# Attention and two MLPs on one core: float64 weights converted in pairs, first MLP cut into even and odd blocks

## The chip, the cores and the metric

The kernel runs on one core of one Trainium2 chip. The metric is the device time of one execution in microseconds (us). The engines are called PE (TensorE), DVE (VectorE), ACT (ScalarE), POOL (GpSimd) and SP (SyncE); SP issues the DMAs of this kernel.

## What is computed

Inputs are `x` (8 batches, 8 heads, 512 rows, 64 columns) and `state` (8, 8, 32, 64), both float32, and four float64 weights. Cross attention in both directions gives 4608 rows of 512; two MLPs without bias follow, one with a squared ReLU, one with ELU:

```python
scores = scale * np.matmul(x, state.transpose(0, 1, 3, 2))
...
xread = np.matmul(a, state)
scores2 = scale * np.matmul(state, x.transpose(0, 1, 3, 2))
...
sread = np.matmul(a2, x)
return np.concatenate([xread, sread], axis=2).astype(np.float32)
...
h = x @ w_in
r = np.maximum(h, 0.0)
g = r * r
return (g @ w_out).astype(np.float32)
...
h = x @ w_in
g = np.where(h > 0.0, h, alpha * (np.exp(np.minimum(h, 0.0)) - 1.0))
return (g @ w_out).astype(np.float32)
```

(What is left out are the two softmaxes, with the maximum subtracted and 1e-9 added to the sum, that give a and a2 from the scores.) In the kernel the weights of the first MLP are `w1` and `v1`, those of the second `w2` and `v2`. A "block" is one batch: 512 rows of `x`; the 32 state rows of all batches are one block of their own.

## The kernel before

**Products.** Every operand of a large matmul is split into a high part (HI, rounded to fp32r) and the rest (LO), and each product is three matmuls, HI·LO, HI·HI and LO·HI (`mm3`, L158 to L160, and `product`, L43). The split is an ACT copy and a DVE subtraction (`split`, L163 and L164).

**Weights.** The four weights arrive as float64 and are turned into float32 on the chip. `load64` loads a raw tile (128 partitions, 512 numbers of 8 bytes, 512 KB) by one DMA on SP, into one of `RAW` = 4 buffers. `convert` needs two ACT steps (L210 on the high words, L212 on the low words) and four DVE steps (L214 clamp, L215 shift, L217 add, L219 sign). A `w1` piece is written into a resident tile. A `v1` piece goes into one of `CV` = 4 buffers `cv`, is stored to DRAM (`d_v`), and is split into a resident tile (L236 on ACT, L238 on DVE).

**Seven products for four.** Where two blocks are taken together, a 2x2 block product is formed from seven products instead of eight (`out_products`, `first_product`). This needs sums of weight blocks, made on DVE (`sums`, into the buffer `tf`, L247 and following), split into `wf` (L260 on ACT, two buffers) and stored to DRAM (`f_w`, `f_v`) by `put_split`; the pair stages load them again as `wr`. For `v1` they are made by `sums_v1` from `d_v` (steps called "f1"), which also stores the split tiles (`p_v`); for `w2` and `v2` by `conv_pair`.

**Stages.** The start: attention of block 0 (scores `sc`, maximum `mx` at L362, exponential at L364, transposes, the operand `at` split at the end), the first `w1` pieces, and small filler matmuls (`idle`, L517). Then blocks 0 to 5 one at a time (`block`): 16 steps f over DFF; each has 6 matmuls `h` from `at` and `m` (the product of `w1` and the state, made by `emit_m` from 16 small matmuls `mp`, L331), relu and square on ACT (L469 to L473) and a DVE subtraction (L474), and, `LAG` = 2 steps later, 12 matmuls `acc` with `v1`. A list `bg` hangs other work on the steps: `next_conv` (a step of each conversion in progress, then perhaps a new one; a load follows when a conversion is over), the attention of the next block, its loads, and the reading of the state (`sr`, `srt`). Block 0 converts `w1` and `v1` while it uses them, and begins the f1 sums; blocks 1 to 5 finish those and convert `w2` and `v2`. Blocks 6 and 7 are a `pair` (h1 in place of h, then `out_products`); the state's rows of the first MLP follow, then the second MLP in four pairs and its state rows.

**Order.** A scheduler orders each engine's instructions by what is written and by estimates of its own; the written order gives priorities. `tc.issue_after` holds an instruction behind another one (`gate`, `pace`). DMAs on SP are issued in SP's order, and each waits for its buffer there.

## Time and profile before

| | us |
|---|---|
| median of 3 runs (lowest, highest) | 1353.0 (1352.66, 1353.6) |
| span of the profiled execution | 1350.5 |
| PE busy | 1327.5 (98%) |
| DVE busy | 951.0 (70%) |
| ACT busy | 839.5 (62%) |
| first h of block 0 / of block 1 | 27.7 / 128.2 |
| first h1 of the pair | 510.7 |

The span is the profiled execution's own time from its first to its last instruction; the runs' time has 2.5 us more around it. A row of the timeline reads: start, duration, engine, line, operation, output<-input, shapes, count, and in brackets the idle time of that engine before it and what ended it. Line numbers are those of the kernel before.

### The profile page before, as it was taken

The numbers are of one execution on the slowest core, as the hardware profiler recorded it, in microseconds if no ns is written. First come the engines' busy times: TensorE is split into PE (matmuls) and PEld (weight loads), VectorE is DVE, ScalarE is ACT, GpSimd is POOL, SyncE is SP. The second block draws the span as 40 slices with busy tenths as digits, with TensorE's granted clock in tenths as the row PEclk, the third lists the DMA queues.
The fourth block names the chain that finished last, engine by engine and source line by source line (L and its number), as shares of the span: only waits on it lengthen the run. The fifth ranks groups of instructions, "written<-read, shape, count | busy, mean of one in ns | idle before, by whom it ended". The sixth has DMA issues, their size and how long they took to land.

```text
span 1350.5 us, 19746 instructions
## 1 busy us (share of the span) xinstructions
PE 1327.5 (98%) x7064; PEld 1057.1 (78%) x7064; DVE 951.0 (70%) x1437; ACT 839.5 (62%) x1417; POOL 0.7 (0%) x6
## 2 busy tenths in 40 slices
PE   8989999999999999999999999999999999999998
PEld 6656777777777776778988888888888888888898
DVE  6997868686878865775576884579636884568644
ACT  5887758676777657644467843676446743666444
POOL 0000000000000000000000000000000000000000
PEclk9999999999999999999999999999999999999999
DMA  6988856575857424279077777767776777778732
GB/s 240 318 300 310 305 178 230 201 267 190 279 197 266 151 82 153 97 255 349 25 252 208 224 240 224 208 194 247 229 225 194 206 210 223 209 204 284 226 110 100
DMA packets 127729, 290.72 MB, mean 215 GB/s; under 512 B 13840, under 2 KB 22032, under 8 KB 124560
## 3 DMA queue, kind: packets, MB, share of 16 engines
q1 hardware_dynamic: 127632, 289.46, 66.3%
q8 instruction: 56, 0.92, 0.3%
q14 instruction: 41, 0.34, 0.1%
HBM read 212.86 MB, written 76.55 MB: 214 GB/s over the span
## 4 chain that ended last, share of the span: by engine, by line
PE 89%; DMA 5%; DVE 3%; ACT 3%; issue 1%; SPq 0%; ACTq 0%; DVEq 0%
PE x L43 16%; PE X L43 13%; PE z L43 8%; PE Z L43 6%; PE acc L158 6%; PE acc L159 6%; PE acc L160 6%; PE h L158 5%; PE h L159 4%; PE h L160 4%; PE y L43 4%; PE Y L43 3%; DMA raw_v<-in_v_dram 2%; PE mp L331 2%; PE hs L43 2%; PE as L43 2%
## 5 line engine op out<-in xcount | busy, mean ns | idle before, releaser
L163 ACT ACTIVATE gp<-g 128x1024 fp32r<-128x1024 f32 (+1 forms) x168 | 154.0, 917 | 146.0 <-PE x L43 69.5
L164 DVE TENSOR_TENSOR gp<-g,gp 128x1024 fp32r<-128x1024 f32 (+1 forms) x168 | 174.9, 1045 | 95.4 <-ACT gp L163 94.4
L43 PE MATMUL x<-gp,wr 128*128 128x512 f32 x960 | 223.5, 390 | 0.0
L43 PEld LDWEIGHTS x<-gp,wr 128*128 128x128 f32 x960 | 179.7, 188 | 39.4 <-ACT eu L71 1.9
L43 PE MATMUL X<-xf,wr 128*128 128x512 f32 x768 | 186.7, 390 | 0.0
L43 PEld LDWEIGHTS X<-xf,wr 128*128 128x128 f32 x768 | 143.4, 188 | 31.7 <-ACT u L748 1.3
L158 PE MATMUL acc<-gs,v 128*128 128x512 f32 x384 | 154.4, 402 | 3.8 <-DVE gs L474 1.9
L159 PE MATMUL acc<-gs,v 128*128 128x512 f32 x384 | 150.4, 392 | 0.0
L160 PE MATMUL acc<-gs,v 128*128 128x512 f32 x384 | 150.2, 392 | 0.0
L43 PE MATMUL z<-gp,wr 128*128 128x512 f32 x480 | 110.4, 389 | 0.0
L744 DVE SCALAR_TENSOR_TENSOR g<-r,g 128x512 f32<-128x512 f32 x96 | 63.9, 689 | 65.8 <-ACT r L743 65.8
L43 PEld LDWEIGHTS z<-gp,wr 128*128 128x128 f32 x480 | 90.1, 188 | 18.7
L158 PE MATMUL h<-at,m 128*128 128x512 f32 x256 | 103.0, 403 | 1.7 <-ACT r L469 1.7
L158 PEld LDWEIGHTS acc<-gs,v 128*128 128x128 f32 x384 | 72.0, 188 | 38.1 <-issue 15.9
L160 PE MATMUL h<-at,m 128*128 128x512 f32 x256 | 100.7, 395 | 0.5 <-ACT m L346 0.5
L159 PE MATMUL h<-at,m 128*128 128x512 f32 x256 | 101.0, 395 | 0.0
L43 PE MATMUL Z<-xf,wr 128*128 128x512 f32 x384 | 97.4, 389 | 0.0
L469 ACT ACTIVATE r<-h 128x512 f32<-128x512 f32 x96 | 57.1, 595 | 64.4 <-PE h L160 64.1
L742 ACT ACTIVATE r<-g 128x512 f32<-128x512 f32 x96 | 57.5, 625 | 57.5 <-DVE g L821 40.4
L160 PEld LDWEIGHTS acc<-gs,v 128*128 128x128 f32 x384 | 72.1, 188 | 19.8 <-issue 4.2
L159 PEld LDWEIGHTS acc<-gs,v 128*128 128x128 f32 x384 | 72.2, 188 | 18.6 <-issue 3.4
L43 PEld LDWEIGHTS Z<-xf,wr 128*128 128x128 f32 x384 | 72.1, 188 | 15.0
(145 smaller groups left out, 2173.6 us busy)
## 6 DMA issues: line engine op xcount, KB each, us to landing
wr<-f_v SPq DMA_DIRECT2D x256, 256.0 KB, 3.0
wr<-f_w SPq DMA_DIRECT2D x224, 256.0 KB, 2.9
f_v<-wf SPq DMA_DIRECT2D x40, 512.0 KB, 3.3
raw_w<-in_w_dram SPq DMA_DIRECT2D x32, 512.0 KB, 4.8
raw_v<-in_v_dram SPq DMA_DIRECT2D x32, 512.0 KB, 5.0
f_w<-wf SPq DMA_DIRECT2D x24, 512.0 KB, 2.8
xt<-in_xt_dram SPq DMA_DIRECT2D x8, 1024.0 KB, 6.9
xn<-in_xn_dram SPq DMA_DIRECT2D x8, 1024.0 KB, 6.1
```

Of the source, the lines that this page charges most:

```text
L43: nc.tensor.matmul(ps, wk[a], xk[b], start=start and k == 0 and i == 0, stop=last and k == len(w) - 1 and i == 2, skip_group_check=True)
L158: mm(ps, w[HI], x[LO], start=first, stop=False)
L159: mm(ps, w[HI], x[HI], start=False, stop=False)
L160: mm(ps, w[LO], x[HI], start=False, stop=last)
L163: copy = nc.scalar.activation(out=hi, in_=src, func=AF.Copy)
L164: nc.vector.tensor_tensor(out=lo, in0=src, in1=hi.bitcast(F32), op=ALU.subtract)
L331: mm(ps[e][32 * k:32 * k + 32, :], st_t[b][r, k, :], x(k, r), start=True, stop=True)
L469: pace[:] = [nc.scalar.activation(out=r, in_=ps, func=AF.Relu)]
L742: act(out=r, in_=h, func=AF.Relu, scale=-1.0)
L744: nc.vector.scalar_tensor_tensor(out=out, in0=r, scalar=-1.0, in1=h, op0=ALU.add, op1=ALU.max)
```

## The change

Raw tiles hold two pieces (1024 numbers, 1 MB), in three buffers instead of four; `cv` holds a pair, two buffers instead of four. The steps of a conversion are half as many and twice as wide, and so are the `v1` splits and the stores `d_v` and `p_v`. The next load is written right behind a conversion's last step. `load_x(0)` comes first, and the first loads are two `w1` pairs and one `v1` pair. Block 0 begins only conversions of `w1` and `v1`; f1 starts in block 1. The sums are made in place in the `cv` tile; `tf` is gone, `wf` has one larger buffer. Of the four blocks that `out_products` works on in the first MLP, two were the lower and upper half of DFF; they are the even and the odd f blocks now, so that the two v1 pieces of one pair belong together. `PLACE` and `columns` say where a form or a column lies, and the host lays out the four weights accordingly.

```diff
-RAW, CV = 4, 4
+RAW, CV = 3, 2
+PLACE = {1: 0, 2: 1, 3: 2, 7: 3, 5: 4, 4: 5, 6: 6}
...
-                  tf=pool("tf", 1),
-                  wf=pool("wf", 2))
-    wo_p = pool("wo", FC)
+                  wf=pool("wf", 1))
+    wo_p = pool("wo", HF)
...
-        def load64(name, i):
+        def load64(name, j):
...
-            t = conv_p["raw"].tile([P, 512, 2], I32, name=f"raw_{name}{i}", tag="raw")
-            nc.sync.dma_start(out=t.rearrange("p f w -> p (f w)"), in_=src64[name][i].bitcast(I32))
+            t = conv_p["raw"].tile([P, 1024, 2], I32, name=f"raw_{name}{j}", tag="raw")
+            nc.sync.dma_start(out=t.rearrange("p f w -> p (f w)"),
+                              in_=src64[name][j].rearrange("p r f -> p (r f)").bitcast(I32))
...
             nc.vector.scalar_tensor_tensor(out=bits, in0=high, scalar=SIGN, in1=bits, op0=ALU.bitwise_and, op1=ALU.bitwise_or)
+            next_load()
...
+        def conv_v1(j):
+            v = conv_p["cv"].tile([P, 2, 512], F32, name="cv", tag="cv")
+            yield from convert("v1", j, v)
+            d = wd["v1", j] = dram.tile([P, 2, 512], F32, name=f"d_v1{j}", tag=f"d_v1{j}")
             nc.sync.dma_start(out=d, in_=v)
-            t = wo_p.tile([P, 2, DM], F32R, name=f"v1_{f}", tag="wo")
+            t = wo_p.tile([P, 2, 2, DM], F32R, name=f"v1_{j}", tag="wo")
...
+        def put_split(w, src):
+
+            n = src.shape[1]
+            h = conv_p["wf"].tile([P, n, 2, 256], F32R, name="wf", tag="wf")
+            with tc.issue_after(pace[0].ins):
+                nc.scalar.activation(out=h[:, :, HI], in_=src, func=AF.Copy)
+            nc.vector.tensor_tensor(out=h[:, :, LO], in0=src, in1=h[:, :, HI].bitcast(F32), op=ALU.subtract)
+            nc.sync.dma_start(out=w, in_=h.bitcast(F32))
+
+        def sums(q):
+
+            b12, b11, b21, b22 = (q[:, i] for i in range(4))
+            sub = lambda out, x, y: nc.vector.tensor_tensor(out=out, in0=x, in1=y, op=ALU.subtract)
+            sub(b11, b12, b11)
+            sub(b12, b22, b12)
+            yield
+            sub(b22, b22, b11)
+            sub(b21, b21, b22)
+            yield
...
+            q = v.rearrange("p r (c f) -> p (r c) f", c=2)
+            put_split(w[:, :3], q[:, 1:])
+            yield
+            yield from sums(q)
+            put_split(w[:, 3:], q)
...
+        def columns(f, k):
+            c = k if f % 2 else (k + 2) % KC
+            return slice(c * P, (c + 1) * P)
+
+        pieces = [("w1", 0), ("w1", 1)]
+        for i in range(HF):
+            pieces += [("v1", i)] + ([("w1", i + 2)] if i < HF - 2 else [])
...
+        def advance():
+            for c in list(busy):
+                if next(c[0], busy) is busy:
+                    busy.remove(c)
+
+        def begin():
+            held = sum(n != "w1" for _, n in busy)
+            if converting and (converting[0][0] == "w1" or held < CV):
...
-        next_load()
         load_x(0)
-        for _ in range(RAW - 1):
+        for _ in range(RAW):
             next_load()
         load_xn(0)
...
+        def first_weights():
+            advance()
+            if converting[0][0] in ("w1", "v1"):
+                begin()
...
             if b == 0:
-                for i in range(FC - 1):
-                    at(i, next_conv)
-                    at(i, next_conv)
+                for i in range(FC + LAG):
+                    at(i, advance)
+                    at(i, first_weights)
...
-                t = g[(11, 12, 21, 22)[s // HF]]
-                if f % 2 == 0:
+                t = g[(11, 12, 21, 22)[s // FC * 2 + f % 2]]
+                if f % 4 < 2:
```

Three places show what this does to the order on the engines. The first is DVE at the very start, the conversion of the first `w1` tile and the maxima `mx0` of block 0's scores. Before:

```order
L214 TENSOR_SCALAR w1_00_154<-w1_00_154 128x512
L215 TENSOR_SCALAR w1_00_154<-w1_00_154 128x512
L217 ISA w1_00_154<-raw_w10_140,w1_00_154 128x1024
L219 SCALAR_TENSOR_TENSOR w1_00_154<-raw_w10_140,w1_00_154 128x512
L362 TENSOR_REDUCE mx0_180<-sc0_0_182 128x1
L362 TENSOR_REDUCE mx0_180<-sc0_1_183 128x1
```

Now:

```order
L213 TENSOR_SCALAR w1_00_149<-w1_00_149 128x1024
L214 TENSOR_SCALAR w1_00_149<-w1_00_149 128x1024
L216 ISA w1_00_149<-raw_w10_141,w1_00_149 128x2048
L218 SCALAR_TENSOR_TENSOR w1_00_149<-raw_w10_141,w1_00_149 128x1024
L361 TENSOR_REDUCE mx0_175<-sc0_0_177 128x1
L361 TENSOR_REDUCE mx0_175<-sc0_1_178 128x1
```

The same four steps stand ahead of `mx0`, on a tile of twice the size; on SP, whose order was raw_w10, st0, xt0, raw_w11, raw_w12, raw_w13, xn0, it is st0, xt0, raw_w10, raw_w11, raw_v10, xn0 now. A little further on DVE's row has the scaling of the state's read-out, `srs0`, ahead of the split of `at0`; it stood in block 0 before.

The second is PE in block 2, the small matmuls `mp3_2` that prepare `m` for block 3, between `h` and `acc`. Before:

```order
L160 MATMUL h_3062<-at3_2548,m3_11_2906 128x512
L331 MATMUL mp3_2_0_3076<-w1_20_489,st3_1574 32x512
L331 MATMUL mp3_2_1_3077<-w1_20_489,st3_1574 32x512
L331 MATMUL mp3_2_0_3076<-w1_20_489,st3_1574 32x512
L331 MATMUL mp3_2_1_3077<-w1_20_489,st3_1574 32x512
L331 MATMUL mp3_2_0_3076<-w1_21_615,st3_1574 32x512
L331 MATMUL mp3_2_1_3077<-w1_21_615,st3_1574 32x512
L331 MATMUL mp3_2_0_3076<-w1_21_615,st3_1574 32x512
L331 MATMUL mp3_2_1_3077<-w1_21_615,st3_1574 32x512
L158 MATMUL acc_2942<-gs_2969,v1_3_484 128x512
```

Now:

```order
L160 MATMUL h_2712<-at3_2244,m3_11_2576 128x512
L330 MATMUL mp3_2_0_2726<-w1_20_466,st3_1334 32x512 x2
L330 MATMUL mp3_2_0_2726<-w1_21_561,st3_1334 32x512 x2
L158 MATMUL acc_2606<-gs_2633,v1_1_416 128x512
L159 MATMUL acc_2606<-gs_2633,v1_1_416 128x512
L330 MATMUL mp3_2_1_2727<-w1_20_466,st3_1334 32x512 x2
L330 MATMUL mp3_2_1_2727<-w1_21_561,st3_1334 32x512 x2
L160 MATMUL acc_2606<-gs_2633,v1_1_416 128x512
```

One group became two, with two `acc` matmuls between them. The scores `sc3`, in the same block range, were split into a first matmul and seven others in the same way; in block 0 the small groups stand in 11 places, where they stood in 14.

The third is ACT where block 5 ends and the pair begins: `o` copies block 5's result, `m6_1` is the first split of the pair's second `m`, `g1` its first relu. Before:

```order
L260 ACTIVATE wf_5176<-tf_4896 128x2x256
L260 ACTIVATE wf_5180<-cv_4789 128x2x256
L503 ACTIVATE o_5196<-acc_4498 128x512
L260 ACTIVATE wf_5208<-tf_5004 128x2x256
L163 ACTIVATE m6_10_5282<-mp6_1_0_5272 128x512
L503 ACTIVATE o_5202<-acc_4500 128x512
L163 ACTIVATE m6_11_5285<-mp6_1_1_5273 128x512
L260 ACTIVATE wf_5212<-tf_5004 128x2x256
L630 ACTIVATE g1_5260<-h1_5253 128x512
```

Now:

```order
L502 ACTIVATE o_4649<-acc_4032 128x512
L502 ACTIVATE o_4655<-acc_4034 128x512
L163 ACTIVATE m6_10_4727<-mp6_1_0_4717 128x512
L163 ACTIVATE m6_11_4730<-mp6_1_1_4718 128x512
L632 ACTIVATE g1_4704<-h1_4697 128x512
```

The `wf` splits of the last weight sums moved to earlier places, and none is left there. On PE the row was mp6_1, mp6_2, h1; it is mp6_1, 36 matmuls of h1, mp6_2.

## Rows read from the trace of the kernel before

**Rows 1.** Page part 1: busy us, share of the span, instructions of each engine.
```profile
PE 1327.5 (98%) x7064; PEld 1057.1 (78%) x7064; DVE 951.0 (70%) x1437; ACT 839.5 (62%) x1417; POOL 0.7 (0%) x6
```

**Rows 2.** Windows: stretch, us, busy PE, PEld, DVE, ACT, POOL, PEclk, DMA share, GB/s.
```profile
9.14:10.00 0.86, 0.86 (x16) 0.18 (x16) 0.00 (x0) 0.00 (x0) 0.00 (x0) 1.00 1.01 414
27.70:128.20 100.50, 92.55 (x516) 59.55 (x515) 90.95 (x180) 83.23 (x153) 0.00 (x0) 0.98 0.88 302
28.30:117.70 89.40, 81.59 (x470) 50.86 (x469) 82.93 (x164) 77.12 (x142) 0.00 (x0) 0.99 0.88 295
128.20:205.00 76.80, 76.80 (x455) 58.48 (x453) 54.38 (x104) 47.91 (x89) 0.00 (x0) 1.00 0.69 245
```

**Rows 3.** Waits of DVE, 28.3 to 117.7: line, releaser, us, times, longest.
```profile
DVE cv L214 <- ACT cv L210: 5.2, 5, 1.3
```

**Rows 4.** Waits of ACT in the same stretch.
```profile
ACT cv L210 <- DMA raw_v<-in_v_dram: 7.5, 5, 2.5
```

**Rows 5.** Timeline of the start: PE, DVE, ACT, SP.
```profile
9.14 1.09 PE L331 MATMUL sc<-xt,st 64*32 64x512 f32 x16 [0.38 <-DMA xt<-in_xt_dram]
...
10.31 1.29 DVE L362 TENSOR_REDUCE mx<-sc 128x1 f32<-128x512 f32 x2 [2.72 <-PE sc L331]
...
18.16 1.06 ACT L376 ACTIVATE t<-t 128x1024 f32<-128x1024 f32 x1 [0.56 <-DVE t L375]
...
30.84 0.69 ACT L210 ACTIVATE cv<-raw_v 128x512 f32<-128x512 f32 x1
...
32.27 1.10 PE L411 MATMUL sr<-xn,a2t 128*32 128x64 f32 x64
...
35.69 0.33 SPq L234 DMA_DIRECT2D d_v<-cv  x1
```

**Rows 6.** Groups by shape, DVE, 28.3 to 117.7: count, busy us, mean ns, idle before.
```profile
L219 DVE SCALAR_TENSOR_TENSOR cv<-raw_v,cv 128x512 int32<-128x512 int32 x16 | 11.0, 685 | 0.1
L238 DVE TENSOR_TENSOR v<-cv,v 128x512 fp32r<-128x512 f32 x16 | 10.9, 682 | 0.0
...
L214 DVE TENSOR_SCALAR cv<-cv 128x512 f32<-128x512 f32 x16 | 6.7, 422 | 5.2 <-ACT cv L210 5.2
...
L375 DVE TENSOR_TENSOR t<-t,m 128x1024 f32<-128x1024 f32 x1 | 1.2, 1217 | 0.0
```

**Rows 7.** Timeline of DVE, two neighbours in the start.
```profile
23.68 1.24 DVE L390 STREAM_TRANSPOSE atf<-t 128x1024 f32<-128x1024 f32 x1
24.84 0.65 DVE L219 SCALAR_TENSOR_TENSOR w<-raw_w,w 128x512 int32<-128x512 int32 x1
```

**Rows 8.** Timeline of PE around a split group in block 0.
```profile
56.32 1.04 PE L331 MATMUL sc<-xt,st 64*32 64x512 f32 x2
57.30 0.74 PE L160 MATMUL h<-at,m 128*128 128x512 f32 x2
```

**Rows 9.** Timeline of PE and ACT at the change from block 5 to the pair.
```profile
504.94 1.09 PE L331 MATMUL mp<-w,st 64*32 64x512 f32 x16
...
505.98 0.63 ACT L260 ACTIVATE wf<-tf 128x512 fp32r<-128x512 f32 x1 [2.37 <-DMA f_v<-wf]
...
507.99 2.81 PE L331 MATMUL mp<-w,st 64*32 64x512 f32 x16 [1.96 <-DVE m L164]
...
510.73 0.79 PE L158 MATMUL h<-at,m 128*128 128x512 f32 x1
...
512.17 0.39 PE L158 MATMUL h<-at,m 128*128 128x512 f32 x1
```

**Rows 10.** Window of the same place, columns as in rows 2.
```profile
508.70:512.10 3.40, 3.40 (x18) 1.38 (x18) 1.38 (x3) 0.14 (x1) 0.00 (x0) 0.51 0.93 357
```

**Rows 11.** DMA issues, 0 to 30, then 30 to 120: count, KB, median us to landing.
```profile
xn<-in_xn_dram SPq DMA_DIRECT2D x1, 1024.0 KB, 11.8
...
raw_v<-in_v_dram SPq DMA_DIRECT2D x14, 512.0 KB, 5.6
...
xn<-in_xn_dram SPq DMA_DIRECT2D x2, 1024.0 KB, 6.5
```

More of the change, by code (lines that the diff above doesn't have):

```diff
@@ L299, in attn_mlp_kernel @@
+        pieces = [("w1", 0), ("w1", 1)]
+        for i in range(HF):
+            pieces += [("v1", i)] + ([("w1", i + 2)] if i < HF - 2 else [])
         pairs2 = [(name, j) for name in ("w2", "v2") for j in range(HF)]
         converting = pieces + [("f1", j) for j in range(HF)] + pairs2
[L301 to L302 removed]
+        loading, busy = iter(pieces + pairs2), []
         def next_load():
@@ L307, in next_load @@
                 load64(*x)
-        def next_conv(more=True):
-            for c, name in list(busy):
-                if next(c, busy) is not None:
-                    busy.remove((c, name))
-                    for _ in range({"w1": 1, "v1": 1, "f1": 0}.get(name, 2)):
-                        next_load()
-            held = sum({"w1": 0, "v1": 1}.get(n, 2) for _, n in busy)
-            if more and converting and (converting[0][0] == "w1" or held + (converting[0][0] != "v1") < CV):
+        def advance():
[5 more added lines that the diff above has]
+            if converting and (converting[0][0] == "w1" or held < CV):
                 name, i = converting.pop(0)
@@ L523, in attn_mlp_kernel @@
         gate.append(A[0]["exp"])
-        for _ in range(3):
-            next_conv()
+        next_conv()
+        advance()
         gate.clear()
@@ L530, in attn_mlp_kernel @@
         at_soft2(0)
-        for _ in range(4):
-            next_conv(False)
+        while busy:
+            advance()
         with busy_pe(8):
```

121 lines of the change are left out of this document (45 added, 76 removed).

## The prediction

> **What bounds the kernel now.** I read the page's busy shares first: PE is busy 1327.5 us of a span of 1350.5 [rows 1], so where PE is full only fewer or shorter matmuls help, and their number stays at 7064. The gain or loss must come from the 23 us in which PE has nothing, or from the price of single PE pieces. Then the windows by stage [rows 2]: block 0, from its first h at 27.7 to block 1's first at 128.2, takes 100.5 us with PE busy 92.55, so 8 of the 23 us lie there; block 1 has no such hole (76.8 of 76.8). In block 0 the engine behind PE is DVE: from 28.3 to 117.7, where the last v1 piece is split, it is busy 82.93 of 89.4 us, PE 81.59, and the DMA share is 0.88. After 117.7 PE is at full pace for the last 10.5 us. So block 0 lasts as long as DVE's chain of conversions plus those 10.5 us. DVE's waits say what is late when DVE stands still: 5.2 of its 6.5 us of idle time are ACT's first conversion step [rows 3], and ACT there waits 7.5 us for raw_v [rows 4]: late loads, passed on. A second place is the change from block 5 to the pair of blocks 6 and 7, below.
>
> **Term 1, the start: +4.0.** Before, the first load is half a megabyte and DVE's four steps on it are over when the scores arrive; PE starts on them at 9.14 as xt lands, and mx follows on DVE at 10.31 [rows 5]. Afterwards w1_00 is 1 MB and third in SP's queue, and DVE's order has its four steps ahead of mx, so mx and all of block 0's softmax wait for it. Until xt lands the queue has moved 1.56 MiB before, and must move 2.06 MiB until w1_00 is in: 0.5 MiB more at the 414 GB/s of that moment [rows 2] is 1.3 us, so it is in at 10.4. ACT's first step on 1024 columns takes 1.06, as on t at 18.16 [rows 5]: 11.5. DVE's four steps on 1024 columns have no rows as such; L219 takes 0.68 on 512 columns and a 1024-wide step of the softmax 1.22 [rows 6], 0.53 more; L217 is taken as L219. L214 takes 0.42 and runs at twice the elements per time, so 0.27 more, 0.69; L215 as L214. Together 0.69 + 0.69 + 1.22 + 1.22 = 3.8, and mx starts at 15.2 instead of 10.3: +4.9. Behind it one pair is converted (3.8) where three pieces were (3 x 2.2 = 6.6): -2.8. The state's read-out sr0 (1.1 on PE at 32.27, [rows 5]), its scaling and its transpose now stand ahead of at0's split and so of the first h; with the hops between the engines, 1.8. Sum +3.9, taken as 4.0; bounds 3.0 (sr0 fits into a wait of PE) and 5.5 (nothing of the 2.8 comes back, since those pieces stood between steps of the softmax that wait for ACT anyway, less what sr0 hides).
>
> **Term 2, block 0: -7.6.** On DVE, 28 conversions of four steps and 16 splits become 14 and 8 of double width. Durations: 28 x (0.42 + 0.42 + 0.68 + 0.685) = 61.7 becomes 14 x 3.81 = 53.3, and 16 x 0.68 = 10.9 becomes 8 x 1.22 = 9.7: 9.6 us less in 64 fewer instructions. But instructions that stand in a row overlap: L390 starts at 23.68 and takes 1.24, and the next starts at 24.84, 1.16 after it [rows 7], so each costs some 0.08 less than its duration, and 64 x 0.08 = 5.1 of the 9.6 were never paid. Net -4.5; in what follows -4.6, as the f1 sums, a step or two of which stand in block 0 now, leave it. Of the idle 6.5 us I take 3.0 away: the f1 transfers (cv<-d_v and p_v<-v) leave block 0, and a load is issued behind the last step of a conversion. Bounds: no idle left, -11.1; the same idle, -4.6; 10 us of idle, -1.1. Below -12.6 PE itself ends it: 92.55 less three splits fewer of its mp pieces (3.2) and sr0's 1.5 that moved ahead is 87.9. Half the idle is in between because the loads are as many bytes as before and each lands later.
>
> The Trainium skill, "VectorE: DVE Perf Modes", section "The TRN2 errata", says that a VectorE operation on SBUF pays a fixed cost per instruction, (N+151)/0.96 ns for an fp32 tensor_tensor, and advises wide tiles. The durations agree (685 and 1217 ns at 512 and 1024 columns [rows 6]); charged in full for each instruction saved, it would give about 10 us here instead of 4.6, and the starts in [rows 7] speak against that.
>
> **Term 3, pieces of PE in blocks 2 and 3: +2.1.** The new order splits two groups of 16 small matmuls that ran whole: the scores in block 2 and the third mp in block 3. A whole group of 16 takes 1.09 [rows 5]. A split-off part costs nearly as much: at 56.32, in block 0, two matmuls of sc take 1.04 and the next h starts 0.98 after them [rows 8], though 2 of 16 would be 0.14. With the first matmul behind it a little longer, 1.07 for each: 2 x 1.07 = 2.1, on PE, which has nothing to hide it. Bounds 1.6 and 2.2.
>
> **Term 4, block 5 to the pair: -4.0.** Behind block 5's last acc, mp6_1 starts at 504.94, and h is at full pace only from 512.17 [rows 9], 7.2 us later, where two mp (1.09 each) and three h (1.44 at half pace from 510.73 on, so 0.7) need 2.9. In between ACT's wf waits 2.37 for the transfer of the wf before it, m6_1 stands behind that wf on ACT, PE waits 1.96 for m, and then runs at 0.51 of its clock, the 1.2 GHz level, from 508.7 to 512.1 [rows 10]. The new order has no wf near m6_1: the last weight sums are long over, and PE goes from mp6_1 to h1. So 7.2 - 2.9 = 4.3; I take 4.0. Bounds -4.3, and -2.0 if a copy of acc keeps m6_1 late enough for the lower clock to return.
>
> **Edits at nothing.** One wf buffer instead of two makes ACT wait for the landing of the previous f transfer in blocks 1 to 4, as it waits 2.37 at 505.98 now [rows 9]; r and gs stand behind it on ACT, and PE's acc behind gs. LAG 2, with two steps of matmuls between h and its acc, covers a wait of that size, and ACT and DVE are busy only 47.91 and 54.38 of 76.8 us in block 1 [rows 2]. If that cover is gone, +2 (one such wait). The exchange of halves and even blocks, PLACE and columns leave numbers, sizes and dependences of the matmuls as they are: 0.
>
> **Sum.** 4.0 - 7.6 + 2.1 - 4.0 = -5.5. The profiled span is 1350.5; the median of the runs, 1353.0, has 2.5 us more around it, which the change doesn't touch. 1353.0 - 5.5 = **1347.5**.
>
> **Rivals.** A: the loads stop holding up DVE, as with twice the bytes per load fewer transfers have to be waited for; with the start at its lower bound, 3.0 - 11.1 + 2.1 - 4.0 = -10.0: 1343.0. For it: three pairs are underway ahead, where four pieces were. Against it: a load's landing grows with its bytes, xn's 1 MB taking 6.5 us and the 512 KB pieces 5.6 [rows 11]. The Trainium skill, "DMA: Bandwidth & Descriptors", section "Bandwidth", asks for 1 MiB and more per transfer to reach three quarters of the peak, which speaks for A; but at 9.14, with half-megabyte loads behind xt, the rate was 414 GB/s already [rows 2].
>
> B: the loads stay as late as they are, and DVE's 6.5 us idle stay, with the start at +5.0: 5.0 - 4.6 + 2.1 - 4.0 = -1.5: 1351.5. The same time comes out if term 4 fails alone. For it: the DMA share of 0.88.
>
> C, slower: the three buffers of 1 MB become the loop that sets block 0. A buffer is free again after landing plus conversion. At my forecast a pair takes 81.8 / 14 = 5.84 us, so a buffer is wanted again after 17.5. Now a piece is held from ACT's first step at 30.84 to the store of its cv at 35.69, 4.9 us [rows 5]; a pair twice that, 9.7. With xn's landing of 6.5 [rows 11] the loop is 16.2 and just fits. With xn's 11.8 in the start [rows 11] it is 21.5. Taken a little over half way, 10.0, it is 19.7: 2.2 more for each of 13 / 3 turns, +9.5: 1357.0. It makes the kernel slower than before by more than 0.2% from a loop of 19.4 on, that is from landings of 9.7. Against it: without f1's transfers block 0 moves fewer bytes.
>
> **How the numbers follow.** Forecast 0.43, A 0.14, B 0.27, C 0.16. Differences within 0.2%, or 2.7 us, are what a measurement of this kernel can't tell from none. Forecast and A lie under 1350.3, but for a little of the forecast's upper end (0.02); B lies within; C above 1355.7. Faster 0.55, same 0.29, slower 0.16. The range reaches from 1342.5, A's time, to 1356.0, short of C.
>
> **What would show it.** Mx at about 15 and the first h at about 32 for term 1 (under 30 would refute it). From the first h to block 1's first, some 93 us for term 2, with about 3.5 us of DVE idle behind ACT's first step; over 100 would be C, with ACT waiting for raw tiles more than the 9 us of now. Two more short groups of L330 in blocks 2 and 3. At the pair, about 3.5 us from the last acc to h at full pace, with no time at the lower clock. The prediction is wrong if ACT's waits for raw_v grow, or if a wait for the one wf buffer puts r behind PE's need in blocks 1 to 4.

## The result and the profile after

The changed kernel takes 1359.84 us (median of 6 runs, 1357.52 to 1365.0) against 1353.3 (6 runs, 1352.23 to 1354.4): a ratio of 1.0056, 95% interval 1.0040 to 1.0072. It is slower by 0.56%, where 1347.5 was forecast; the time lies above the range of 1342.5 to 1356.0. The profiled execution took 1359.61, with a span of 1357.8, 7.3 more than before.

Where the 7.3 us of span arise is read from PE's timeline: the first h of each block in both kernels (us from the span's start).

| | before | after | gained (-) or lost (+) in the stretch that ends here |
|---|---|---|---|
| first h of block 0 | 27.73 | 29.98 | +2.25 (forecast +4.0) |
| first h of block 1 | 128.20 | 128.39 | -2.06 (forecast -7.6) |
| first h of block 2 | 202.38 | 202.57 | 0.00 |
| first h of block 5 | 424.92 | 435.30 | +10.19 (forecast +2.1) |
| last acc of block 5 ends | 505.01 | 515.11 | -0.28 |
| first h of the pair | 510.73 | 516.91 | -3.92 (forecast -4.0) |
| first X of the second MLP | 691.12 | 697.22 | -0.08 |
| last matmul | 1345.91 | 1353.26 | +1.25 |

(Block 1's first h is that of [rows 2]; the last window there, to 205.00, reaches 2.6 us into block 2.) So the loss is made in blocks 2 to 4, where the kernel before had no hole. The +1.25 in the second MLP is left out of what follows: the stretch from the first X to the state's last rows took 586.6 us in the kernel before, e1, e3 and e4 below, and 587.8 to 588.1 in the changed kernel, e7 and e14, with the same instructions there in all of them. The three longer ones have a stretch at the lower clock where that MLP begins, and the four shorter ones have none; in the changed kernel it is this window (columns of [rows 2]), behind a wait of 2.25 us for a weight. It is not the whole answer, as e2 took 587.8 us there without one.

```profile
696.50:700.00 3.50, 3.34 (x8) 2.70 (x9) 3.29 (x3) 0.46 (x1) 0.00 (x0) 0.51 0.93 300
```

Page part 1 of the changed kernel, to be held against [rows 1]: fewer and longer instructions on DVE and ACT, and PE busy 2.5 us more with the same 7064 matmuls.

```profile
PE 1330.0 (98%) x7064; PEld 1060.8 (78%) x7064; DVE 941.3 (69%) x1261; ACT 833.8 (61%) x1305; POOL 0.7 (0%) x6
```

The start, from the timeline of the changed kernel, against [rows 5]: w1_00 is in at 8.8, its four steps come ahead of mx, and mx starts at 13.96. Xt, issued at 1.18, took 5.1 us to land (last line, DMA issues from 0 to 14), so it was in at 6.3; PE came to the scores only at 8.72, behind its filler matmuls.

```profile
8.72 1.09 PE L330 MATMUL sc<-xt,st 64*32 64x512 f32 x16
...
8.81 1.16 ACT L209 ACTIVATE w<-raw_w 128x1024 f32<-128x1024 f32 x1 [6.48 <-DMA raw_w<-in_w_dram]
...
10.00 0.69 DVE L213 TENSOR_SCALAR w<-w 128x1024 f32<-128x1024 f32 x1 [10.00 <-ACT w L209]
...
12.82 1.23 DVE L218 SCALAR_TENSOR_TENSOR w<-raw_w,w 128x1024 int32<-128x1024 int32 x1
13.96 1.28 DVE L361 TENSOR_REDUCE mx<-sc 128x1 f32<-128x512 f32 x2
...
xt<-in_xt_dram SPq DMA_DIRECT2D x1, 1024.0 KB, 5.1
```

Block 0, windows with the columns of [rows 2]: from its first h to block 1's, and DVE's stretch of conversions, which answers to 28.30 to 117.70 there.

```profile
29.98:128.39 98.41, 88.65 (x449) 59.37 (x449) 83.19 (x108) 79.20 (x111) 0.00 (x0) 0.97 0.84 296
...
30.65:118.00 87.35, 77.59 (x401) 50.24 (x400) 78.10 (x99) 73.03 (x103) 0.00 (x0) 0.96 0.83 288
```

DVE is busy 78.10 us there instead of 82.93, and idle 9.25 instead of 6.5. What DVE waited for, and what ACT did, against [rows 3, 4]:

```profile
DVE w L213 <- ACT w L209: 2.7, 2, 2.1
DVE cv L213 <- ACT cv L209: 2.2, 1, 2.2
DVE gs L473 <- ACT gs L472: 1.6, 3, 1.1
```

```profile
ACT m L343 <- PE mp L330: 6.1, 2, 4.5
ACT cv L209 <- DMA raw_v<-in_v_dram: 2.0, 1, 2.0
ACT w L209 <- DMA raw_w<-in_w_dram: 1.6, 2, 0.9
```

ACT's wait for raw_v is down from 7.5 us to 2.0 (its second step, on the other word, waits 1.3 more for the same tile), but a wait for m's small matmuls, up to 4.5 at once, has come.

Blocks 2 to 4 as one window, first the kernel before, then the changed one:

```profile
202.38:424.92 222.54, 222.54 (x1327) 169.24 (x1326) 171.80 (x330) 158.82 (x297) 0.00 (x0) 1.00 0.65 228
```

```profile
202.57:435.30 232.73, 228.75 (x1328) 170.41 (x1326) 181.59 (x277) 162.09 (x256) 0.00 (x0) 0.99 0.67 243
```

Before, PE was busy all of the 222.54 us. Now it takes 10.2 us more: 4.0 of waiting and 6.2 of longer busy time for the same matmuls. Of the 6.2, the two groups that are split now are 2.0, the lower clock in block 3 (below) is 1.7, and a third mp group, which takes 2.19 us in block 4 where a whole one takes 1.09, is 1.1. DVE has 9.8 us more to do in this stretch. Counted by the splits into `wf` on ACT, the sums of 14 pairs of w2 and v2 stand in it (28 wide splits, two for each pair), where it was 12 (48 narrow ones, four for each). PE's waits in it, and ACT's for DMAs:

```profile
PE acc L158 <- DVE gs L473: 1.6, 2, 1.2
PE acc L158 <- ACT o L502: 1.0, 1, 1.0
PE mp L330 <- DVE t L365: 0.9, 1, 0.9
PE sc L330 <- DVE m L164: 0.4, 1, 0.4
```

```profile
ACT raw_v L211 <- DMA raw_v<-in_v_dram: 9.1, 6, 3.0
ACT raw_w L211 <- DMA raw_w<-in_w_dram: 7.9, 3, 4.4
ACT wf L245 <- DMA f_w<-wf: 5.5, 5, 2.0
```

The waits of PE are few, short and of four kinds. ACT's waits for raw tiles are no news by themselves: in the kernel before they came to 14.2 us in the same blocks, with 2.4 more for wf, while PE never waited:

```profile
ACT raw_v L212 <- DMA raw_v<-in_v_dram: 7.8, 6, 2.4
ACT raw_w L212 <- DMA raw_w<-in_w_dram: 6.4, 6, 2.4
```

One of PE's waits as an example, in block 3 (timeline of PE):

```profile
301.68 0.40 PE L159 MATMUL acc<-gs,v 128*128 128x512 f32 x1
302.98 1.06 PE L330 MATMUL mp<-w,st 64*32 64x512 f32 x8 [0.90 <-DVE t L365]
303.97 0.79 PE L160 MATMUL acc<-gs,v 128*128 128x512 f32 x1
304.56 0.63 PE L158 MATMUL acc<-gs,v 128*128 128x512 f32 x1
...
307.12 0.54 PE L158 MATMUL acc<-gs,v 128*128 128x512 f32 x1
307.50 0.39 PE L159 MATMUL acc<-gs,v 128*128 128x512 f32 x1
```

Here the second half of the split mp3_2 waits 0.90 us for a transpose that DVE makes late; then seven matmuls take 0.63 or more instead of 0.39, and the granted clock is 0.66 of full speed on average over 303 to 308: part of that stretch ran at the lower of its two levels, 1.2 GHz, and the rest at 2.4.

At the pair (timeline of PE), against [rows 9]: h1 follows mp6_1 with a wait of 0.78, at full pace.

```profile
515.04 1.09 PE L330 MATMUL mp<-w,st 64*32 64x512 f32 x16
516.91 0.50 PE L158 MATMUL h<-at,m 128*128 128x512 f32 x1 [0.78 <-ACT o L502]
517.25 0.40 PE L159 MATMUL h<-at,m 128*128 128x512 f32 x1
```

### The profile page after: what moved, and what is told of

The parts are those of the page before. It is cut to its first block, busy times and chain, and to the rows that moved or that the text cites. A ratio compares the mean times of both kernels' runs of the same rounds, so it can differ in the third digit from the quotient of the medians.

```text
span 1357.8 us, 19168 instructions
## 1 busy us (share of the span) xinstructions
PE 1330.0 (98%) x7064; PEld 1060.8 (78%) x7064; DVE 941.3 (69%) x1261; ACT 833.8 (61%) x1305; POOL 0.7 (0%) x6
## 4 chain that ended last, share of the span: by engine, by line
PE 86%; ACT 4%; DMA 4%; DVE 3%; issue 1%; SPq 0%; ACTq 0%; DVEq 0%
PE x L44 16%; PE X L44 13%; PE z L44 8%; PE Z L44 6%; PE acc L158 6%; PE acc L160 5%; PE acc L159 5%; PE h L158 4%; PE y L44 4%; PE h L160 4%; PE h L159 4%; PE Y L44 3%; PE mp L330 2%; PE hs L44 2%; PE as L44 2%
## 5 line engine op out<-in xcount | busy, mean ns | idle before, releaser
L158 PE MATMUL acc<-gs,v 128*128 128x512 f32 x384 | 157.3, 410 | 10.4 <-ACT v L233 5.1
L158 PEld LDWEIGHTS acc<-gs,v 128*128 128x128 f32 x384 | 72.9, 190 | 50.4 <-issue 16.8
L473 DVE TENSOR_TENSOR gs<-g,gs 128x512 fp32r<-128x512 f32 x96 | 65.7, 684 | 38.8 <-ACT gs L472 34.2
L160 PEld LDWEIGHTS acc<-gs,v 128*128 128x128 f32 x384 | 73.5, 192 | 20.4 <-issue 4.2
L159 PEld LDWEIGHTS acc<-gs,v 128*128 128x128 f32 x384 | 73.3, 191 | 14.7 <-issue 0.8
```

The source lines that it names most:

```text
L158: mm(ps, w[HI], x[LO], start=first, stop=False)
L159: mm(ps, w[HI], x[HI], start=False, stop=False)
L160: mm(ps, w[LO], x[HI], start=False, stop=last)
L473: nc.vector.tensor_tensor(out=gs[:, LO], in0=g, in1=gs[:, HI].bitcast(F32), op=ALU.subtract)
```

## Experiments

"Blocks 2 to 4" is the time from block 2's first h to block 5's, "block 0" that from its first h to block 1's. Ratios are to the kernel before, with the 95% interval. The block times come from one profiled execution each; blocks 1 to 3 took the same 74.2 us each in the kernel before and in e12 and e14, which have the same work there. Where PE waits, they repeat less well: e8, in which PE, DVE and ACT have the changed kernel's order in blocks 1 to 4, took 0.7 us less for blocks 2 to 4 and up to 1.7 less in one block, and the runs of the changed kernel spread over 7.5 us. A difference of some 3 us between two such executions is therefore weak evidence.

Four things were open: what costs blocks 2 to 4 their 10.2 us (one wf buffer, late loads, a denser background, or wide steps), why block 0 gained 2.1 and not 7.6, whether the start is the order of mx, and whether the gain at the pair can be had in the kernel before.

**e1, two wf buffers.**

```diff
-                  wf=pool("wf", 1))
+                  wf=pool("wf", 2))
...
+            for c in range(0, src.shape[1], 2):
+                x = src[:, c:min(c + 2, src.shape[1])]
```

> The changed kernel with wf as two buffers of half the size, its splits and stores cut into pieces of at most two forms as before; nothing else is edited (the scheduler's order follows). Theory W (one wf buffer makes ACT wait for the store of the piece before, with r and gs of the blocks behind it): blocks 2 to 4, 232.7 us now from block 2's first h to block 5's, fall to 222 to 226, near the 222.5 before; block 0 stays near 98; the time falls by 7 to 10, to about 1351. Theory L (1 MB loads into three buffers come late and hold up ACT in all blocks): the waits for raw tiles stay, blocks 2 to 4 stay above 229, the time falls by at most 3, to 1357 or more.

1358.7 us, ratio 1.0055 (1.0034 to 1.0076).

```profile
202.98:432.86 229.88, 224.01 (x1327) 168.90 (x1326) 181.55 (x303) 163.35 (x283) 0.00 (x0) 1.00 0.68 242
```

Blocks 2 to 4 take 229.9, 2.9 less than in the changed kernel. Theory W (222 to 226) is out, and the numbers of L (above 229, and 1357 or more) came. But L's reason doesn't follow from them: ACT's waits for raw tiles and wf are 12.2 us there, less than the 16.6 of the kernel before, and PE still waits 5.9.

**e2, narrow steps.** Each of the steps of `convert` runs over `out[:, :512]` and then `out[:, 512:]`:

```diff
-            nc.vector.tensor_tensor(out=bits, in0=bits, in1=low, op=ALU.add)
+            for s in parts:
+                nc.vector.tensor_tensor(out=bits[:, s], in0=bits[:, s], in1=low[:, s], op=ALU.add)
```

> The changed kernel with 1 MB loads, but each step of a conversion done in two instructions of 512 columns. Theory N (merging the steps is what gave block 0 its 2 us, by the 0.08 us of overlap that an instruction costs less than its duration): DVE's busy time in block 0 rises by some 4 us from 78, its idle time stays near 9, block 0 takes 102 or so instead of 98.4, the time is 4 higher. Rival G (the wide steps are too coarse: ACT and DVE wait for each other and PE waits for gs and v behind 1.2 us steps): the idle time of DVE falls by as much as its busy time rises, block 0 stays at 97 to 99. Under either, blocks 2 to 4 keep their 230, as wf is as in the changed kernel.

1361.15 us, ratio 1.0051 (1.0034 to 1.0068).

```profile
31.06:132.13 101.07, 91.89 (x448) 58.44 (x449) 86.57 (x164) 81.09 (x141) 0.00 (x0) 0.98 0.83 288
```

Block 0 is 2.7 us longer than in the changed kernel and DVE busy 3.4 us more, while its idle time falls only from 15.2 to 14.5. Theory N holds for block 0: the width of the steps is worth about 3 us there, and it isn't what leaves DVE idle. The whole time, which N put 4 us higher, is not higher by its ratio (1.0051, and 1.0056 for the changed kernel). Blocks 2 to 4 take 229.5, 3.2 less than in the changed kernel, though wf and the steps per pair are as they were.

**e3, loads of 512 KB.**

```diff
+            for r in range(2):
+                nc.sync.dma_start(out=t[:, r * 512:(r + 1) * 512].rearrange("p f w -> p (f w)"),
+                                  in_=src64[name][j][:, r].bitcast(I32))
```

> The changed kernel with each raw tile loaded by two transfers of 512 KB into its halves, everything else as it is. If the size of one transfer matters for block 0's waits: with a cost per transfer that is not hidden, 14 pairs cost some 1 to 2 us each more in landing and block 0 grows by 3 or more; if a large transfer itself lands late because it is large, block 0 shrinks. If only the bytes and the number of buffers count, block 0 and the time stay within 1.5 us of the changed kernel.

1358.96 us, ratio 1.0040 (1.0026 to 1.0055). Block 0 takes 97.9 us, against 98.4: the size of a transfer makes no difference there. Blocks 2 to 4 took 227.9; since this profiled execution was the fastest of the kernel's runs (1354.89 to 1360.69), nothing is built on that.

**e4, the kernel before with its sums earlier.**

```diff
-                    if i % (9 if nb < SINGLE else 3):
-                        at(i, next_conv)
+                    at(i, next_conv)
```

> The kernel before with a conversion step hung on each of the 18 steps of blocks 1 to 5, instead of leaving out every ninth (and every third in block 5), so that the last weight sums are over well ahead of the pair. Theory of the prediction's term 4: the 7.2 us from mp6_1 to h at full pace become about 3, and the time falls by 4, to 1349. Rival: the denser steps cost in blocks 1 to 4 what the transition gives, and the time stays within 1.5 us of the kernel before.

1355.07 us, ratio 1.0012 (1.0001 to 1.0023). The last sums are stored at 451.9 instead of 509.6, and from acc's end to h1 it is 1.9 us instead of 5.7. But blocks 1 to 4, which took 296.7, take 300.5, and block 0 and the start 1.1 more. Theory's 1349 is missed, and the rival is right that the denser steps cost what the pair gains (the time rose by 1.8, where it allowed 1.5). In blocks 2 to 4, 54 narrow splits, or 13.5 pairs, stand where it was 12, and these blocks take 3.4 us more: background that arrives in full blocks costs PE time there without any other edit of the change.

**e5, the low words behind the high words.** ACT's second step stood far ahead of the first one, right behind the landing of the raw tile.

```diff
-                nc.scalar.activation(out=out, in_=high.bitcast(F32), func=AF.Copy, scale=2.0 ** -112)
-            with tc.issue_after(gate[0].ins) if gate else nullcontext():
+                first = nc.scalar.activation(out=out, in_=high.bitcast(F32), func=AF.Copy, scale=2.0 ** -112)
+            with tc.issue_after(first.ins):
```

> The changed kernel with ACT's second conversion step (low words, L211) held behind the first step (high words, L209) of the same pair; it stood ahead of it, right behind the landing of the raw tile. Theory R (ACT, in order, waits there for a 1 MB load that nothing needs yet, up to 4.4 us at once, and r and gs of the block behind it come late for PE): ACT's waits for raw tiles in blocks 2 to 4, 17.0 us now, fall under 3, blocks 2 to 4 take 225 to 229 instead of 232.7, the time falls by 4 to 7, to about 1354. Rival P (the background is denser, as a pair needs fewer steps and the weight sums are over 32 us earlier than before): blocks 2 to 4 stay at 231 or more and the time stays within 2 us of 1359.8.

1361.76 us, ratio 1.0059 (1.0039 to 1.0079). ACT's waits for raw tiles are gone from its list of waits in blocks 2 to 4, but these take 235.6 us: PE now waits for other things, 2.5 for o and 2.3 for r, and ACT 19.3 for wf, where it waited 7.9 in the changed kernel. Theory R fell: a wait of ACT for loads is not by itself what PE pays. Rival P's expectation (231 or more, within 2 us of 1359.8) held.

**e6, both edits.** The edits of e1 and e5 together.

> Both edits: the low step behind the high step, and two wf buffers of half the size. If ACT's waits for DMAs (raw tiles and wf together) are what PE pays in blocks 2 to 4, these fall to 222.5 to 224, as before the change, the time to 1350 to 1352, and block 0 and the pair's start stay as in the changed kernel (98.4, and 1.8 from acc's end to h1). Rival P, density: blocks 2 to 4 stay at 228 or more.

1363.9 us, ratio 1.0073 (1.0051 to 1.0096); blocks 2 to 4 take 234.1. P's expectation (228 or more) held, and the theory's times fell. But the run doesn't test the theory's condition: the waits for raw tiles are gone, while ACT still waits 11.7 us for wf and 5.0 for the transfer of o, and PE 7.5.

**e7, e4 with the low step behind the high step.** The edits of e4 and e5 on the kernel before.

> The kernel before with a conversion step on all 18 steps of blocks 1 to 5 and the low step held behind the high step. Theory R: what the denser steps alone lost in blocks 1 to 4 (3.7 us) was ACT's wait for raw tiles, and goes; the gain at the pair (3.8 us) stays; the time is 1349 to 1350. Rival P: the loss in blocks 1 to 4 stays above 2.5 us and the time is 1353 or more.

1352.56 us, ratio 0.9994 (0.9982 to 1.0006): no difference to the kernel before. Blocks 1 to 4 take 299.6, 2.9 more than before (all of it in blocks 2 to 4), where e4 lost 3.8; the gain at the pair stays. R's 1349 to 1350 is missed; the loss that P expected in blocks 1 to 4 (over 2.5) is there, though its time (1353 or more) is just missed.

**e8, mx first.**

```diff
+            with tc.issue_after(A[0]["mul"].ins) if (name, j) == ("w1", 0) else nullcontext():
+                nc.vector.tensor_scalar(out=out, in0=out, scalar1=CLAMP, scalar2=-CLAMP, op0=ALU.min, op1=ALU.max)
```

> The changed kernel with DVE's first conversion step of the first w1 tile held behind the two maxima of block 0's scores. Theory (term 1): mx starts at about 10 instead of 13.96, and the first h comes 1.5 to 3 us earlier, at 27 to 28.5. Rival: m of block 0 needs both w1 tiles converted, that work only moves behind the softmax's first steps, and the first h stays within 0.7 us of 29.98. The rest of the kernel is as in the changed one; the time falls by as much or stays.

1359.3 us, ratio 1.0040 (1.0028 to 1.0053). Mx starts at 9.03, 4.9 earlier, and the first h comes at 29.65, 0.33 earlier. The rival holds: the conversion of w1 is needed before the first h, and it only changes its place. Blocks 2 to 4, in the same order as in the changed kernel, take 232.1 (232.7 there).

**e9, wf and pace.** e1, and each piece of `put_split` on a step of its own, so that a pair of w2 or v2 is spread over 10 steps; by the code it was 9 before the change (the expectation's "as many steps as before" is one off) and 8 after it. An f1 sum takes 3 steps, where it was 5 and then 4. There are 18, 16, 16, 16 and 18 steps in blocks 1 to 5.

```diff
+            for c in range(0, src.shape[1], 2):
+                yield
...
-                    if i % (9 if nb < SINGLE else 3):
+                    if i % 9 or nb in (2, SINGLE):
```

> The changed kernel with two wf buffers of half the size and each piece of at most two forms on a step of its own, so that a pair of w2 or v2 takes as many steps as before; all 18 steps of blocks 1 and 5 are used, so that the sums still end before the pair. Theory P (what PE loses in blocks 2 to 4 comes from a background that is denser than before: more of it per step of a block): blocks 2 to 4 take 222.5 to 225 us instead of 232.7, the time falls to 1350 to 1352. Rival S (the shapes: steps of 1024 columns and loads of 1 MB on engines that run in order, whatever the pace): blocks 2 to 4 stay at 229 or more, and the time at 1357 or more.

1355.44 us, ratio 1.0013 (1.0004 to 1.0022): 4.4 less than the changed kernel.

```profile
208.71:432.81 224.10, 223.65 (x1328) 169.21 (x1327) 164.87 (x268) 152.92 (x266) 0.00 (x0) 1.00 0.58 207
```

Blocks 2 to 4 take 224.1, as theory P said, with wide steps and 1 MB loads: 8.6 of the 10.2 us are back, and DVE has 164.87 us to do there instead of 181.59. P's time, 1350 to 1352, is missed, and so are both numbers of S (229 or more, 1357 or more). Two things limit what this shows. Block 1, which had 18 steps and DVE busy 61.7 us instead of 52.4, takes 78.0 instead of 74.2, so that blocks 1 to 4 together take 302.1: 4.8 less than in the changed kernel, and 5.4 more than before. And blocks 2 to 4 hold 43 narrow splits, 10.75 pairs, fewer than the 12 of the kernel before: part of the 8.6 has only moved with the work.

**e10, the same steps in the middle of the blocks.**

```diff
-                    if i % (9 if nb < SINGLE else 3):
+                    if nb < SINGLE and 3 <= i < 16 or nb == SINGLE and i % 3:
                         at(i, next_conv)
+                    if nb < SINGLE and i in (6, 9, 12):
+                        at(i, next_conv)
```

> The changed kernel with the same 16 conversion steps in each of blocks 1 to 4, but all on steps 3 to 15 (three of them twice), none where one block ends and the next begins. Theory B (PE's stalls come where blocks meet, as o, the copy that frees acc, stands behind conversion work on ACT and DVE): blocks 2 to 4 fall by 5 or more, to 228 or less, and PE no longer waits for o. Theory P: the doubled steps stall PE in the middle of the blocks instead, and blocks 2 to 4 stay at 231 or more.

1364.81 us, ratio 1.0082 (1.0068 to 1.0096); blocks 2 to 4 take 235.2. Theory B fell, and P's expectation (231 or more) held.

**e11, two raw buffers.** `RAW, CV = 2, 2`.

> The changed kernel with two raw buffers of 1 MB instead of three. Rival C of the prediction (block 0 is set by the loop of landing and conversion, three buffers being too few): with two, a buffer must come round in two pairs' time, 11.7 us, where landing and conversion need 15 or more, and block 0 grows from 98.4 to 110 or more. If the loop isn't what sets block 0: within 4 us of 98.4.

1366.46 us, ratio 1.0096 (1.0082 to 1.0111).

```profile
30.51:133.67 103.16, 87.57 (x449) 60.09 (x450) 84.43 (x108) 78.82 (x110) 0.00 (x0) 0.95 0.83 287
```

Block 0 grows by 4.8, between the two expectations: the loads have a share in its length, but the loop that rival C worked out would have given 11 or more.

**e12, the kernel before with a full block 5.** `if i % 9 or nb == SINGLE`, so that block 5 has 18 steps instead of 12, and the others keep theirs.

> The kernel before with a conversion step on all 18 steps of block 5 (12 of 18 before) and nothing else. Blocks 0 to 4 keep their order and their times (h of block 5 at 424.9 within 0.5 us); the last weight sums are over before acc of block 5 ends. Term 4 of the prediction: 3.5 to 4.2 us less from acc's end to h at full pace, the time 1349 to 1349.8, faster than both kernels. Rival: the denser steps stall PE inside block 5 by as much, and the time is 1352 or more.

1355.74 us, ratio 1.0014 (1.0002 to 1.0026). Block 5 with the start of the pair, before and in e12 (windows):

```profile
424.92:510.73 85.81, 82.97 (x565) 58.91 (x563) 64.24 (x119) 55.80 (x106) 0.00 (x0) 0.99 0.45 158
```

```profile
427.74:513.54 85.80, 80.61 (x550) 58.23 (x548) 61.17 (x116) 54.50 (x105) 0.00 (x0) 1.00 0.44 160
```

From acc's end to h1 it is 1.9 us instead of 5.7, as term 4 says; inside block 5 PE waits 4.1 us for the split of m on DVE, and the sum is the same to 0.01. Term 4's time (1349 to 1349.8) is missed and the rival's (1352 or more) came. Blocks 1 to 4 kept their order, but h of block 5 came 2.8 us later than the 424.9 expected, 1.5 of them in block 0.

**e13, pace, with f1's sums in block 0 again.** e9's `put_split`; `first_weights` begins any conversion; 16 steps in blocks 1 to 4, 13 in block 5.

```diff
-            if converting[0][0] in ("w1", "v1"):
-                begin()
+            begin()
```

> The changed kernel with e9's two half-size wf buffers and steps per pair, with f1's sums allowed at the end of block 0 as before the change, 16 steps in blocks 1 to 4 and 13 in block 5, so that the weight sums end shortly ahead of the pair. Theory P (what a block loses depends on how much background is put on its steps): block 1, which lost 3.9 us under 18 steps in e9, takes 74 to 75.5 again, blocks 2 to 4 222.5 to 225.5, the pair's start keeps its gain of 3.9, and with the start's +2.3 and block 0 between -2 and +1 the time is 1350 to 1354, beside 1353.1 before. Rival S (shapes): blocks 1 to 4 lose 4 or more against 296.7 before and the time is 1356 or more.

1361.96 us, ratio 1.0070 (1.0056 to 1.0084). Blocks 3 and 4 take 75.0 and 74.2, but block 1 takes 78.0 and block 2 82.5. P is right for two blocks and wrong for two, and its time (1350 to 1354) is missed. Blocks 1 to 4 lose 13.0 and the time is over 1356, as rival S had it, with 11.25 pairs in blocks 2 to 4.

**e14, the kernel before with five raw buffers.** `RAW, CV = 5, 4`.

> The kernel before with five raw buffers of 512 KB instead of four. If block 0's idle time of DVE (6.5 us before, 9.2 after) is the loop of landing and conversion through too few buffers: the idle time falls under 3.5 and block 0 takes 97.5 or less instead of 100.5. If it is the order of ACT, which waits for m's small matmuls and for gs while conversions stand behind: block 0 stays within 1.5 us of 100.5.

1350.28 us, ratio 0.9986 (0.9976 to 0.9996): the only kernel here whose interval lies below 1: faster than the one before by 0.14%, if by little more than the noise, and so faster than both. Block 0 takes 100.3 us in the profiled execution, as before, so in the kernel before the buffers are not what leaves DVE idle there; as that execution was the slowest of its ten runs (1354.3), it doesn't show where the 2.3 us come from.

**e15, evenly spread.** e9 with `if i % (18 if nb < SINGLE else 9)`: 17 steps in blocks 1 to 4, 16 in block 5.

> As e9 (two wf buffers of half the size, a pair of w2 or v2 in as many steps as before), with the steps spread evenly: 17 in each of blocks 1 to 4 and 16 in block 5, where e9 had 18, 16, 16, 16, 18. Over all kernels so far, blocks in which DVE is busy 57.4 us or less took 74.2 to 75.2 us, and blocks with 58.8 or more took 74.2 to 82.5. Theory P: with DVE at 55 to 58 us in each of blocks 1 to 4 these take 74.2 to 76 each, 297 to 301 together (296.7 before, 306.9 after the change, 302.1 in e9), and the time is 1352 to 1354.5. Rival S, or that the order of the engines alone decides by chance: some block of the four still loses 3 us or more, and the time is 1356 or more.

1354.74 us, ratio 1.0015 (1.0005 to 1.0024). Blocks 3 and 4 take 74.3 and 74.5; block 1 takes 76.6 (DVE busy 61.2) and block 2 79.2, with DVE busy 56.6, less than in a block before the change. P's 297 to 301 for blocks 1 to 4 is missed (304.5); of rival S, a block that loses 3 us came (block 2, 5.0), and the time of 1356 or more did not. So a low load of DVE in a block as a whole doesn't exclude a stall: a wait of 1.66 us ends at 228.45, for z from DVE, after two of sixteen small matmuls, and a stretch at the lower clock follows (0.83 on average from 226 to 236).

```profile
225.78 1.01 PE L332 MATMUL mp<-w,st 64*32 64x512 f32 x2
228.45 1.26 PE L332 MATMUL mp<-w,st 64*32 64x512 f32 x14 [1.66 <-DVE z L415]
229.64 0.79 PE L158 MATMUL acc<-gs,v 128*128 128x512 f32 x1
230.23 0.63 PE L159 MATMUL acc<-gs,v 128*128 128x512 f32 x1
```

**e16, the pace alone.** The changed kernel with `if b in (1, SINGLE - 1) or i % 4`: 13 steps in blocks 2 to 4, 18 in blocks 1 and 5.

> The changed kernel with its pace alone altered: 13 conversion steps in blocks 2 to 4 (16 before), 18 in blocks 1 and 5 (16 and 12); one wf buffer, wide steps and 1 MB loads stay. Pace: DVE's work in blocks 2 to 4 falls from 60.5 to some 55 us each, and these blocks take 222.5 to 227 us (232.7 in the changed kernel, 229.9 with two wf buffers alone, 224.1 in e9 with both); the pair's start keeps its gain; the time is 1353 to 1357. If it is the wf buffer together with the pace, or the shapes: 229 or more, and 1357 or more.

1360.88 us, ratio 1.0061 (1.0038 to 1.0084).

```profile
205.05:434.81 229.76, 225.45 (x1328) 168.87 (x1326) 166.01 (x256) 154.34 (x249) 0.00 (x0) 1.00 0.59 210
```

Blocks 2 to 4 take 229.8 with 24 wide splits, the 12 pairs of the kernel before, and with less work on DVE than there (166.01 us, and 171.80 before): they still lose 7.2, so the amount of background in these blocks is not by itself what PE pays. The expectation's other branch (229 or more, and 1357 or more) came; it doesn't part the wf buffer together with the pace from the shapes. In one execution each, blocks 2 to 4 get back 3.0 by the pace alone, 2.9 by the second wf buffer alone (e1), 3.2 by narrow steps alone (e2), and 8.6 by pace and wf together (e9).

## Why the prediction was wrong

**The step that failed is the one called "edits at nothing".** Of the 12.8 us between the forecast and the measured span, 8.1 arise in blocks 2 to 4, 5.5 in block 0 (term 2) and 1.25 in the second MLP, and the start was 1.75 better than forecast. The smaller wf pool was put at 0, at most +2, and that a pair of w2 or v2 now takes fewer of `next_conv`'s steps (8 instead of 9) was not seen at all. The work moved into blocks 2 to 4, 14 pairs of sums instead of 12, where DVE has 181.59 us to do instead of 171.80, and out of block 5. The cover was read from block 1, with DVE busy 54.38 us, and not from blocks 2 to 4, where it was 57.3 in each already. These blocks had no hole to hide anything in, as PE was busy 222.54 of 222.54 us before, and they lost 10.2 us, 2.0 of them the split groups of term 3.

What the runs show of the cause is a part. Background that arrives in full blocks costs PE time there: in the kernel before, with nothing else edited, 13.5 pairs instead of 12 cost 3.4 us in blocks 2 to 4 (e4), and e12 lost in block 5 what it gained at the pair. And in the changed kernel two half-size wf buffers and a slower pace (10 steps for a pair) together bring the ratio from 1.0056 to 1.0013 (e9) and 1.0015 (e15), clear of the intervals, where neither alone moves it (1.0055 in e1, 1.0061 in e16).

That these two are the cause of the 10.2 us is not shown. e13 has both, with f1's sums begun in block 0, and is no faster than the changed kernel (1.0070); over blocks 1 to 4 e9 still takes 5.4 us more than before, e15 7.8 and e13 13.0; and e16 has the 12 pairs of before and still loses 7.2 in blocks 2 to 4. The wide steps and the large loads, rival S, are not excluded: no run has narrow steps or half loads together with e9's wf and pace, and narrow steps alone gave back as much in blocks 2 to 4 (e2) as the wf buffer or the pace alone. Nor is it settled which wait ends late in a given block. ACT's waits for loads are not it by themselves, as they were 14.2 us in the kernel before and gone in e5; in e5, e6 and e10 PE waits 5.1, 7.5 and 7.4 us, for other things than the 4.0 of the changed kernel. So the greater part of the 10.2 us stays open.

**Term 4 was right in itself and wrong in the sum.** From acc's end to the pair's first h it is 1.8 us instead of 5.7, -3.9 for -4.0. But the sums had left the pair's start by being done earlier, and the prediction booked their leaving and not their coming. e12 is this in its purest form: 3.8 us gained at the pair, 3.8 lost in block 5; e4 is the same over blocks 1 to 4.

**Term 3** forecast 2.1 for two more pieces. They are there, the sc in block 2 and the mp in block 3, and their own price is the forecast one, 1.04 and 0.96. In block 3 the second piece also waited 0.90 for DVE and was followed by three microseconds at the lower clock, so that this one cost some 3.6 instead of 1.07: 0.96 for the piece, 0.90 of wait, and 1.7 more because the eight matmuls that start from 303.97 to 307.12 took 3.5 us (to the next start at 307.50) instead of 1.8. The lower clock was no part of the forecast.

**Term 2** was half right. DVE's work fell by 4.8 us (82.93 to 78.10) for a forecast of 4.6, and e2 shows the width of the steps behind it; the discount of 0.08 us for each instruction was needed, since without it 9.6 had been forecast. That is also where this case differs from the Trainium skill, "VectorE: DVE Perf Modes", section "The TRN2 errata", if its fixed cost is charged for every instruction saved. The idle time rose to 9.25 where 3.5 was forecast, 5.75 off, by a choice half way between ends that the rows did not support: with [rows 4] gone from 7.5 to 2.0, ACT waits 6.1 for m's matmuls (2.4 before), and DVE waits for ACT. One reason given for less idle time, that the f1 transfers leave block 0, did not come about: six of the eight stores p_v, now of 1 MB, and two of the loads cv<-d_v are still issued there, where ten stores of 512 KB and seven loads of half the size were, and block 0 moves 29.12 MB, not much less than the 30.39 of before. That the size of a transfer is not the cause is shown by e3; for the number of buffers there is e14, in the kernel before alone, and e11 (+4.8 with one buffer fewer). That it is the order on ACT is only argued from the rows. PE also has two stretches at the lower clock in block 0 now (granted clock 0.50 from 48.0 to 51.4 and from 99.2 to 102.6), where the kernel before has none after 30.9; what they cost block 0 is not shown.

**Term 1** had the right sign and was too large, +2.25 for +4.0. The first step on w1_00 starts at 8.81 on ACT, where 10.4 was worked out. The sum kept 9.14, xt's time in the kernel before, and set the load 1.3 us behind it; but xt, now ahead of all raw tiles, was in at 6.3, and w1_00 2.5 us behind it. Mx is 3.65 later, not 4.9. From mx to the first h it is 16.0 us instead of 17.4, -1.4 where -1.0 stood. e8 shows that the order of mx and the conversion costs some 0.3 of it.

**The rivals.** C named the right side with the wrong mechanism: its loop was to lengthen block 0, which became shorter, and e11 says that even two buffers give less than half of it. A and B both kept the blocks after block 0 as the forecast had them, so no case of the prediction held the one that came. The lower end of the range, 1342.5, lies half a microsecond under A's 1343.0, whose time it is said to be. The upper end of the range, 1356.0, was C's price less a microsecond; a case for "the work that leaves the pair arrives in full blocks" would have read its price from the busy share of blocks 1 to 4.

## What to carry to other kernels

Work that a change takes out of one place arrives in another: look up how busy the bottleneck engine is there, and if it has no hole, book a cost. Where a background runs in steps that are hung on the foreground's loop, fewer or larger steps change its pace; here two half-size buffers and a slower pace helped together (1.0013 and 1.0015 for 1.0056) and neither alone did, though a third kernel with both gained nothing. When an edit moves work to another place, count the loss there too: blocks 2 to 4 of e9 got 8.6 us back, and block 1 gave up 3.8 of them. Before merging small instructions into wide ones, count what the small ones overlap: here half of the saved durations had never been paid.

## What the hardware showed beyond the forecast

Two 1 MB transfers issued one after the other on SP, xt at 1.18 and w1_00 at 1.65, landed one after the other: xt at 6.3, w1_00 at 8.8, 2.5 us apart, which is what 1 MiB takes at the rate of that moment (410 GB/s from 7 to 8).

A wait of PE of 0.90 us, between small matmuls in block 3, was followed by some three microseconds at the lower clock, and one of 1.66 us in e15 likewise; before, none of blocks 1 to 4 shows this (granted clock 1.00 throughout). The length of a wait doesn't decide it: the changed kernel's wait of 1.22 us for gs, which ends at 278.42 in block 2, was followed by full speed (granted clock 1.00 from 276 to 286):

```profile
278.42 0.50 PE L158 MATMUL acc<-gs,v 128*128 128x512 f32 x1 [1.22 <-DVE gs L473]
```

In block 3 the 0.90 us of wait and the 1.7 us that the slower matmuls took more make 2.6 us, nearly three times the wait. It is not what costs blocks 2 to 4 most: e8 and e11 have no stretch at the lower clock in them and take 232.1 and 232.3.

The wide steps took what was worked out from [rows 6]: 0.69 us for the clamp and the shift and 1.22 to 1.23 for the add and the sign, on 1024 columns.
